# Clustered attention, mixture of experts and a rational layer on one core: first logits kept in PSUM, early weight loads and routing steps placed anew

## The chip, the cores and the metric

The kernel runs on one core of a Trainium2 chip. Its engines are TensorE (PE; the loads of its stationary operand are listed as PEld), VectorE (DVE), ScalarE (ACT), GpSimd (POOL) and SyncE (SP), which issues most DMAs. The metric is the time of one execution on the device, in microseconds (us). All texts below count from the first instruction of the profiled execution.

## The reference: what is computed

Three layers follow each other; all values are float32.

```python
# 1. attention: B=2, H=8, S=768, D=64, 16 clusters for each head
q_assign = argmax(normalize(q) @ normalize(centroids).T)   # likewise k_assign
scores = where(q_assign[:, None] == k_assign[None, :], q @ k.T / sqrt(D), -1e9)
x = softmax(scores) @ v                                    # to [1536, 512]
# 2. top-1 mixture of experts: E=8, d=512, f=1024
e = argmax(normalize(x) @ normalize(expert_emb).T / tau)
x = gate * (relu(x @ w1[e]) @ w2[e])
# 3. a layer of 2048 with a rational function P/Q between its products
h = x @ w_in
out = (P(h) / (Q(h) + 1e-6)) @ w_out
```

## The kernel before

Every product with weights is made of three matmuls in fp32r: a value is split in a rounded high part and a remainder, and high x high, high x low and low x high are added. The split of a weight chunk (1 MB, `[128, 4, 512]`) goes by quarters: `split_to` (L108) casts the quarter on ScalarE (L110) and subtracts on VectorE (L113).

**The blocks.** The program is written in three blocks under `tc.manual_schedule()`: attention (L642 to L812), experts (L1058 to L1102) and last layer (L1167 to L1192). Within a block each engine's instructions are issued as they are written. The timeline shows that instructions of a later block can be issued ahead of an earlier block's.

**Attention.** 16 heads of two halves make 32 *units*; a unit has 6 *slots*, one for each block of 128 keys, so the loop at L778 has 192 slots and a tail of 6. In a slot TensorE transposes three 128x128 blocks of probabilities (`transp`, `pt`, L428), ScalarE and VectorE split them (`phi` L436, `plo` L446), and TensorE multiplies with values (`pv`, L456 and L457). Other work is put into slots by hand with `at(slot, function)`: the scores of a later unit (`scores`, L410 and L411, then the maximum `nm`, L413, and `expo`, L419), the preparation of a later head, and the storing of `w_in` and `w_out` in another order by way of `words` (word_load, word_low, word_high, word_join, word_store). At the end of a unit `finish` multiplies with an identity and the expert embeddings (`px`, L488).

**A head's preparation.** With w = 12 i - 29 for head i: at slot w - 4 `prep_split` splits keys and queries and starts two moves between partitions (`KB<-QA`, `QB<-KA`); at w + 1 `prep_swap` starts two more, of which the second (`QA<-QA`) overwrites what the first (`KA<-QA`) reads; the clusters' logits, maxima and one-hot follow (`cl_logits` to `cl_onehot`), and at w + 14 `cl_transp` transposes the one-hot and moves it into the operands (`KB<-ot`, `QB<-ot`), where it adds the mask to the scores, which begin at w + 21. All of these moves are DMAs within the chip and go through SyncE's queue, which is in order.

**The start.** The first two heads are prepared ahead of the loop (L696 to L712). Their logits `pl` (`cl_logits_first`, a PSUM tile under the tag of `pt`) are copied to SBUF by ScalarE (`cl_copy_first`, L338); VectorE then subtracts the maximum (L357), scales and adds an index (L359), takes the maximum again (L367) and subtracts (L371). `cl_transp_first(0)` transposes the one-hot of head 0; ScalarE copies it to `KB` and VectorE to `QB` (L395).

**Weights of the experts.** `plan` has 32 chunks, four for each expert: w1 in two halves, then w2 in two halves. `weights(count)` (L161) issues loads into one of three raw buffers (`wraw`, L123) up to two chunks ahead of the one being split, and splits `count` quarters. In the attention loop `weights(0)` is put at slot 130: three loads, no split. The second block begins with `load_x(0)` (the gather of the first expert's rows, a DMA by GpSimd, L842), `weights(8)` (chunks 0 and 1, with the loads of 3 and 4) and `transpose_x(0)`. Chunk 1's ring buffer is that of `words` until the last word is read.

**Routing.** When three blocks of tokens are finished, `route(b, g)` (L511), a generator of nine steps, finds their experts, ranks and rows. `advance()` (L637) takes the first running generator one step on: once in a unit (the slot with kb = 2), twice in each slot from 186 on. In a step the rank matmul reads `cum`, the count by expert so far; the ninth step multiplies `at_row` with `J` (`rJ`, from GpSimd) into `ptab` and adds to `table` and `cum`. The table gives the gather its row numbers (`row_tok`).

**Experts.** For each expert and pair p of 128 columns: `expert_in` (24 matmuls, L959), `weights(3)`, `expert_relu` (ACT L966, DVE L968), `expert_out` of the pair before (L982 to L984), `weights(3)`.

Of the kernel before, what the change touches and what calls it, by code (L numbers as in the profile page):

```python
# [10 lines left out]
F32 = mybir.dt.float32  # L11
# [10 lines left out]
P = 128  # L22
# [6 lines left out]
def attention_moe_kernel(ctx: ExitStack, tc: tile.TileContext, kqT, vp, centroids,  # L29
# [37 lines left out]
    def move(dst, src):  # L67
        sp.dma_start(dst.bitcast(F32), src.bitcast(F32))
# [51 lines left out]
    def prep_f32(key, src, tag):  # L120

        raw = stage.tile([P, 4, 512], F32, name="wraw", tag="wraw")
        sp.dma_start(raw, src)  # L123
        yield
        ck = new_chunk(key, tag)
        for i in range(4):
            split_to(ck, i, raw[:, i], act, dve)
            yield
# [29 lines left out]
        e, c = divmod(n - RING, 4)  # L158
        return n < RING or (("in", "in", "out", "out")[c], e, 2 * (c % 2) + 1) in passed

    def weights(count):  # L161

        while place["chunk"] < len(plan):
            n, ahead = place["chunk"], place["loaded"]
            if ahead < len(plan) and ahead <= n + 2:
                next(plan[ahead])
                place["loaded"] += 1
                continue
            if count == 0 or not free(n):
                return  # L170
            next(plan[n])
            count -= 1
            place["quarter"] += 1
            if place["quarter"] == 4:
                place["chunk"] += 1
                place["quarter"] = 0

# [118 lines left out]
    def prep_swap(i):  # L298
        hi, lo = st[i]["QA"], st[i]["KA"]
        move(lo[D:P], hi[0:D])  # L300
        move(hi[0:D], hi[D:P])

    def prep_split_first(i, qk):
# [27 lines left out]
    def cl_logits_first(i):  # L331
        pl = pT.tile([P, NB, 2 * C], F32, name="pl1", tag="pt")
        for blk in range(NB):
            pe.matmul(pl[:, blk, :], st[i]["kq"][:, blk * P:(blk + 1) * P], CB[:, heads[i][1], :],
                      start=True, stop=True)
        st[i]["pl"] = pl

    def cl_copy_first(i):  # L338
        st[i]["L"] = hp.tile([P, G, C], F32, name="L")
        act.copy(st[i]["L"].rearrange("p (b a) c -> p b (a c)", a=2), st[i].pop("pl"))  # L340

    def cl_logits(i):
        pl = pM.tile([P, NB, 2 * C], F32, name="pl", tag="pm")
# [6 lines left out]
    def cl_max(i):  # L350
        st[i]["mx"] = sm.tile([P, G, 1], F32, name="mx")
        dve.tensor_reduce(st[i]["mx"], st[i]["L"], axis=AX.X, op=ALU.max)
# [35 lines left out]
    def cl_transp_first(i):  # L388

        po = [pS.tile([C, 1024], BF16, name="po1", tag="ps") for a in range(2)]  # L390
        for a in range(2):
            for blk in range(NB):
                pe.transpose(po[a][:, blk * P:(blk + 1) * P], st[i]["ohb"][:, blk, a, :], identb)
        act.copy(KBs[i % NSET][0:C], po[0][:, :S])  # L394
        dve.tensor_copy(QBs[i % NSET][0:C], po[1][:, :S])  # L395
# [115 lines left out]
    def route(b, g):  # L511
# [45 lines left out]
        rk = rE("rrk")  # L557
        dve.tensor_tensor(rk, oh, pr, op=ALU.mult)
        dve.tensor_reduce(rank, rk, axis=AX.X, op=ALU.add)
        yield  # L560

        second = r3("rsec")
        dve.tensor_scalar(second, rank, float(P), None, op0=ALU.is_ge)
        row = r3("rrow")
        dve.scalar_tensor_tensor(row, second, -float(P), rank, op0=ALU.mult, op1=ALU.add)
        at_row = xpool.tile([P, 3, P], F32R, name="at_row", bufs=1)
        dve.tensor_tensor(at_row, iotp.unsqueeze(1).to_broadcast([P, 3, P]),
                          row.to_broadcast([P, 3, P]), op=ALU.is_equal)
        J = xpool.tile([P, 3, E, 2], F32R, name="rJ")
# [5 lines left out]
               pM.tile([P, E * 2], F32, name="ptab", tag="pm"))  # L575
        for j in range(3):
            pe.matmul(pt_, at_row[:, j, :], J[:, j].rearrange("p e t -> p (e t)"), start=(j == 0), stop=(j == 2))
        cs = xpool.tile([P, E], F32, name="rcs")
        dve.tensor_reduce(cs, ohb.rearrange("p j e -> p e j"), axis=AX.X, op=ALU.add)
        if last:  # L580
            dve.tensor_tensor(row_tok, table, pt_, op=ALU.add)
        else:
            dve.tensor_tensor(table, table, pt_, op=ALU.add)
        dve.tensor_tensor(cum, cum, cs, op=ALU.add)


    n = len(units)
# [3 lines left out]
    def at(slot, fn, *args):  # L591
        tasks.setdefault(max(slot, 0), []).append((fn, args))
# [3 lines left out]
    for i in range(2, NH):  # L596
        w = (i - 2) * 2 * NB - 5
        if i > 2:
            at(w + -4, prep_split, i)
            at(w + 1, cl_logits, i)  # L600
            at(w + 1, prep_swap, i)
        at(w + 1, cl_max, i)
        at(w + 4, cl_rank, i, dve if i == 2 else pool)
        at(w + 7, cl_first, i)
        at(w + 8, cl_diff, i, dve if i == 2 else pool)
        at(w + 9, cl_onehot, i)
        at(w + 14, cl_transp, i)
        at(w + 16, prep_v, i)
        if i + 2 < NH:
            at(max(w + 7, 9), prep_load, i + 2)  # L610
# [31 lines left out]
    with tc.manual_schedule():  # L642
# [26 lines left out]
        load_v(2)  # L669

        dve.memset(half, 0.5)
        junk = hp.tile([P, DM], F32, name="junk", bufs=1)
        acc = const.tile([P, 4], F32, name="acc")
        make_identity(nc, ident)
        dve.memset(CB, 0.0)
# [16 lines left out]
            pool.memset(t[0:D].bitcast(F32), 0.0)  # L692
        prep_split(1)
        prep_swap(1)
        prep_split_first(0, qk)
        cl_logits_first(0)  # L696
        cl_logits_first(1)
        cl_copy_first(0)
        cl_max(0)
        cl_rank(0, dve)  # L700
        cl_first(0)
        cl_diff(0, dve)
        prep_split(2)
        cl_onehot(0)
        cl_copy_first(1)
        norm_1(embs, E, junk[:E, :], acc[:E, 2:3])
        cl_max(1)
        cl_rank(1, dve)
        cl_transp_first(0)
        cl_first(1)  # L710
        cl_diff(1, dve)
        cl_onehot(1)  # L712
# [8 lines left out]
        expo(0, 2)  # L721
        cl_logits(2)
        prep_swap(2)
        expo(1, 0)

        def rest_1():
# [46 lines left out]
        for slot, fn in ((42, constants_1), (48, constants_2), (61, constants_3), (73, constants_4)):  # L773
            at(slot, fn)
        at(1, prep_load, 3)
        at(130, weights, 0)

        for t in range(T + 6):  # L778
            u, kb = divmod(t, NB)
            todo = tasks.pop(t, [])  # L780
            if t < T:
                transp(u, kb)
            for fn, args in todo:
                if fn is word_high:
                    fn(*args)
            for fn, args in todo:
                if fn is expo:
                    fn(*args)
            if t < T:
                transp_lo(u, kb)  # L790
            if t >= NB and kb == 4 and u - 1 not in FK:
                finish(u - 1)
                i, g = units[u - 1]
                if heads[i][1] == H - 1:
                    begin(route(heads[i][0], g))
            for fn, args in todo:
                if fn is not expo and fn is not word_high:
                    fn(*args)
            if t >= 2 and t - 2 < T and (t - 2) % NB:
                pv((t - 2) // NB, (t - 2) % NB)  # L800
            if t >= NB and kb == 1:
                pv(u - 1, 0)
                pv_out(u - 1)
            if t >= NB and kb == FK.get(u - 1):
                finish(u - 1)
                i, g = units[u - 1]
                if heads[i][1] == H - 1:
                    begin(route(heads[i][0], g))
            for _ in range(2 if t >= T - NB else kb == 2):
                advance()  # L810
        while running:
            advance()  # L812

    px_.close()
    xstack.close()
# [241 lines left out]

    with tc.manual_schedule():  # L1058
        load_x(0)
        weights(8)  # L1060
        transpose_x(0)
        later = [row_gates(0), positions()]
        next(later[0])
        steps = [(e, p) for e in range(E) for p in range(FB // 2)]
# [257 lines left out]
```

## Time and profile before

| | |
|---|---|
| runs | 781.44, 782.83, 788.40 us; median 782.83 |
| profiled execution | 782.98 us, of which the span from first to last instruction is 781.3 |
| mean granted TensorE clock | 0.982 of full |
| PE, PEld busy | 736.7, 643.2 us |
| DVE, ACT, POOL busy | 597.3, 566.2, 352.2 us |
| DMA | 109.22 MB, 140 GB/s in the mean |

A row of the timeline names the start, the duration, engine, line and operation, the tile written and the tiles read, and in brackets how long the engine was idle before and what ended that. "x6" merges six of a kind. A table by windows has, for each stretch, the time in which each engine was busy and its number of instructions, the mean granted clock of TensorE (1.00 is full), and the share of time in which the DMA engines were busy. Waits are listed as who waited for whom, with the sum, the number and the longest.

### The profile page before, as it was taken

How to read it: one execution, taken by the hardware profiler on the slowest of the kernel's cores; microseconds unless marked ns; L12 is line 12 of the kernel's file. 1: busy time of each engine (PE TensorE's matmuls, PEld its weight loads, DVE VectorE, ACT ScalarE, POOL GpSimd, SP SyncE). 2: the span in 40 equal slices, each digit the busy share in tenths (PEclk: the TensorE clock that was granted, in tenths of full speed). 3: DMA queues.
4: the chain of work that ended last, by engine and by line, in shares of the span. 5: the costliest groups of instructions: out<-in, count | busy, mean ns of one | idle time of the engine just before them, and what ended most of it. 6: DMA issues, size and time to landing. Idle time of an engine off the chain costs nothing. (4 is left out here: it accounts for less than half of the span.)

```text
span 781.3 us, 12623 instructions
## 1 busy us (share of the span) xinstructions
PE 736.7 (94%) x4292; PEld 643.2 (82%) x4292; DVE 597.3 (76%) x1120; ACT 566.2 (72%) x1132; POOL 352.2 (45%) x448
## 2 busy tenths in 40 slices
PE   5999999999979975999999999999999999999995
PEld 4799999989869964988999899878788888888884
DVE  7788888889867993888656564598987878787774
ACT  3788888888868862777755565588887777777773
POOL 7498888878765523021110112066544432242212
PEclk9999999999999995999999999999999999999998
DMA  5566776778877332699655746222100200010001
GB/s 150 154 198 177 215 210 185 228 198 264 268 204 212 100 127 81 229 322 314 210 197 201 267 157 219 86 67 96 29 0 11 73 17 11 1 54 1 1 0 58
DMA packets 48313, 109.22 MB, mean 140 GB/s; under 512 B 6921, under 2 KB 10505, under 8 KB 48242
## 3 DMA queue, kind: packets, MB, share of 16 engines
q1 hardware_dynamic: 45042, 97.74, 40.4%
q0 software_dynamic: 3200, 10.60, 4.3%
q8 instruction: 36, 0.59, 0.3%
q14 instruction: 35, 0.29, 0.1%
HBM read 76.06 MB, written 18.99 MB: 122 GB/s over the span
## 5 line engine op out<-in xcount | busy, mean ns | idle before, releaser
L1054 POOL TENSOR_TENSOR Bt<-Bt,A 128x512 f32<-128x512 f32 x46 | 59.6, 1296 | 146.5 <-ACT Bt L1052 146.5
L446 DVE TENSOR_TENSOR plo<-pt,phi 128x384 fp32r<-128x384 f32 x160 | 88.0, 551 | 23.1 <-ACT phi L436 20.7
L436 ACT CAST phi<-pt 128x384 fp32r<-128x384 f32 x160 | 76.7, 483 | 35.4 <-PE pt L428 34.3
L413 DVE TENSOR_REDUCE nm<-ps 128x1 f32<-128x768 f32 x96 | 91.3, 951 | 10.5 <-PE ps L411 10.1
L428 PE MATMUL pt<-ident,pr 128*128 128x128 f32 x576 | 96.6, 277 | 2.4 <-DVE plo L446 2.1
L1027 PE MATMUL pg<-x2hi,ck 128*128 128x512 f32 x368 | 92.5, 393 | 2.4 <-DVE Ct L1055 2.4
L113 DVE TENSOR_TENSOR ck<-wraw,ck 128x512 fp32r<-128x512 f32 x128 | 82.3, 694 | 14.4 <-ACT ck L110 14.4
L419 ACT ACTIVATE pr<-ps,nm 128x768 f32<-128x768 f32 x96 | 87.4, 911 | 1.9 <-DVE nm L413 1.3
L1027 PEld LDWEIGHTS pg<-x2hi,ck 128*128 128x128 f32 x368 | 68.9, 188 | 18.7 <-DVE Ct L1055 3.3
L428 PEld LDWEIGHTS pt<-ident,pr 128*128 128x128 f32 x576 | 72.2, 141 | 14.3 <-DVE plo L446 6.0
L1151 PE MATMUL pr<-ck,ghi 128*128 128x512 f32 x192 | 75.9, 395 | 0.0
L1153 PE MATMUL pr<-ck,glo 128*128 128x512 f32 x192 | 75.4, 393 | 0.0
L1152 PE MATMUL pr<-ck,ghi 128*128 128x512 f32 x192 | 75.1, 391 | 0.0
L110 ACT CAST ck<-wraw 128x512 fp32r<-128x512 f32 x128 | 71.2, 623 | 5.3 <-DMA wraw<-in_w_dram 5.2
L410 PE MATMUL ps<-KA,QA 128*128 128x384 f32 x192 | 74.4, 388 | 0.6 <-ACT KB L394 0.4
L456 PE MATMUL po_acc<-phi,vhl 128*128 128x384 f32 x192 | 74.1, 386 | 0.0
L959 PE MATMUL ph<-xhi,ck 128*128 128x256 f32 x512 | 73.3, 287 | 0.7 <-ACT xhi L946 0.7
L959 PEld LDWEIGHTS ph<-xhi,ck 128*128 128x128 f32 x512 | 69.1, 194 | 3.6 <-ACT xhi L946 1.1
L411 PE MATMUL ps<-KB,QB 128*128 128x384 f32 x192 | 66.9, 348 | 5.3 <-DMA QB<-ot 3.7
L852 POOL TENSOR_TENSOR gss<-gss,half 128x2 f32<-128x2 f32 x8 | 5.8, 721 | 144.4 <-ACT px L851 144.4
L457 PE MATMUL po_acc<-plo,vhl 128*128 128x384 f32 x192 | 65.3, 340 | 0.0
L1128 DVE SCALAR_TENSOR_TENSOR Bt<-Bt,A 128x512 f32<-128x512 f32 (+1 forms) x48 | 32.7, 682 | 37.3 <-ACT A L1127 37.0
(252 smaller groups left out, 1847.1 us busy)
## 6 DMA issues: line engine op xcount, KB each, us to landing
wraw<-in_w_dram SPq DMA_DIRECT2D x32, 1024.0 KB, 6.7
words<-in_w_in_dram SPq DMA_DIRECT2D x16, 512.0 KB, 3.9
wf_d<-wz SPq DMA_DIRECT2D x32, 256.0 KB, 2.3
words<-in_w_out_dram SPq DMA_DIRECT2D x16, 512.0 KB, 6.0
yraw<-wf_d SPq DMA_DIRECT2D x16, 512.0 KB, 3.7
kq<-in_kqT_dram SPq DMA_DIRECT2D x16, 384.0 KB, 4.2
ys_d<-ysb SPq DMA_DIRECT2D x16, 260.0 KB, 6.4
v<-in_vp_dram SPq DMA_DIRECT2D x16, 192.0 KB, 5.4
```

Source lines behind the costliest of these rows:

```text
L113: el.tensor_tensor(ck[:, 1, i], src, ck[:, 0, i].bitcast(F32), op=ALU.subtract)
L410: pe.matmul(o, d["QA"][:, q0:q0 + P], d["KA"][:, nh * HS:(nh + 1) * HS], start=True, stop=False)
L413: dve.tensor_reduce(nm, ps[:, :, :HS], axis=AX.XY, op=ALU.max, negate=True)
L419: act.activation(pr.rearrange("p (a s) -> p a s", a=2), ps[:, :, :HS], AF.Exp, bias=nm[:, 0:1], accum_out=st["sum", u][:, qb:qb + 1])
L428: pe.transpose(t[:, j, :], st["P", u][j][:, kb * P:(kb + 1) * P], ident)
L436: act.copy(phi, tv)
L446: dve.tensor_tensor(plo, tv, phi.bitcast(F32), op=ALU.subtract)
L959: pe.matmul(ph[:, f2, :], w[:, wx, k, c0:c0 + P], x[:, k, :], start=(i == 0), stop=(i == len(ops) - 1))
L1027: pe.matmul(ph, w[:, wx, k, c0:c0 + P], x[:, k, :], start=(i == 0), stop=(i == len(ops) - 1))
L1151: pe.matmul(o, ghi[:, s_], w[:, 0, k, :], start=(fb == 0), stop=False)
L1152: pe.matmul(o, ghi[:, s_], w[:, 1, k, :], start=False, stop=False)
L1153: pe.matmul(o, glo[:, s_], w[:, 0, k, :], start=False, stop=(fb == F2B - 1))
```

## The change

The logits of heads 0 and 1 stay in PSUM, where VectorE works on them in place, and the one-hot of head 0 is transposed ahead of head 1's `cl_rank`. The second move of a swap is issued three slots later. The first three weight loads are issued at slots 131, 143 and 155. Chunk 0 is split at the end of the first block; the second block gathers and transposes x, then issues the load of chunk 3 from ScalarE's queue and splits chunk 1. Two routing generators advance in the same step, and `cum` is brought up to date before the ninth step, except in the last group.

```diff
@@ prep_f32
-        sp.dma_start(raw, src)
+        (act if key == ("w2", 0, 1) else sp).dma_start(raw, src)
@@ weights
-    def weights(count):
+    def weights(count, loads=2):
-            if ahead < len(plan) and ahead <= n + 2:
+            if ahead < len(plan) and ahead <= n + loads:
+    def load_ahead(n):
+        assert place["loaded"] == n
+        next(plan[n])
+        place["loaded"] += 1
@@ prep_swap
         move(lo[D:P], hi[0:D])
+
+    def prep_swap_2(i):
+        hi = st[i]["QA"]
         move(hi[0:D], hi[D:P])
@@ cl_logits_first
-        st[i]["pl"] = pl
-
-    def cl_copy_first(i):
-        st[i]["L"] = hp.tile([P, G, C], F32, name="L")
-        act.copy(st[i]["L"].rearrange("p (b a) c -> p b (a c)", a=2), st[i].pop("pl"))
+        st[i]["L"] = pl.rearrange("p b (a c) -> p (b a) c", a=2)
@@ route
+        def count():
+            cs = xpool.tile([P, E], F32, name="rcs")
+            dve.tensor_reduce(cs, ohb.rearrange("p j e -> p e j"), axis=AX.X, op=ALU.add)
+            dve.tensor_tensor(cum, cum, cs, op=ALU.add)
+
+        if not last:
+            count()
         yield
...
-        at_row = xpool.tile([P, 3, P], F32R, name="at_row", bufs=1)
+        at_row = xpool.tile([P, 3, P], F32R, name="at_row", bufs=2)
...
-        cs = xpool.tile([P, E], F32, name="rcs")
-        dve.tensor_reduce(cs, ohb.rearrange("p j e -> p e j"), axis=AX.X, op=ALU.add)
         if last:
             dve.tensor_tensor(row_tok, table, pt_, op=ALU.add)
+            count()
         else:
             dve.tensor_tensor(table, table, pt_, op=ALU.add)
-        dve.tensor_tensor(cum, cum, cs, op=ALU.add)
@@ preparation of the heads, in the loop over i
             at(w + 1, prep_swap, i)
+            at(w + 4, prep_swap_2, i)
@@ first block
-        junk = hp.tile([P, DM], F32, name="junk", bufs=1)
+        junk = words["z"][5].bitcast(F32)
...
         prep_swap(1)
+        prep_swap_2(1)
         prep_split_first(0, qk)
         cl_logits_first(0)
         cl_logits_first(1)
-        cl_copy_first(0)
         cl_max(0)
...
-        cl_copy_first(1)
         norm_1(embs, E, junk[:E, :], acc[:E, 2:3])
         cl_max(1)
+        cl_transp_first(0)
         cl_rank(1, dve)
-        cl_transp_first(0)
...
         prep_swap(2)
+        prep_swap_2(2)
...
-        at(130, weights, 0)
+        for j in range(3):
+            at(131 + 12 * j, load_ahead, j)
...
-                advance()
+                advance(2)
         while running:
             advance()
+        weights(4, 1)
@@ second block
         load_x(0)
-        weights(8)
         transpose_x(0)
+        load_ahead(3)
+        weights(4)
```

## Rows read from the trace of the kernel before

**Rows 1.** The page: busy time by engine over the span.
```profile
PE 736.7 (94%) x4292; PEld 643.2 (82%) x4292; DVE 597.3 (76%) x1120; ACT 566.2 (72%) x1132; POOL 352.2 (45%) x448
```
**Rows 2.** Busy time by windows: steady attention, its middle, the hand-over.
```profile
core 0: us, PE busy (x) PEld busy (x) DVE busy (x) ACT busy (x) POOL busy (x), PEclk, DMA share, GB/s
39.10:55.10 16.00, 15.99 (x115) 14.90 (x114) 13.53 (x26) 13.89 (x32) 14.68 (x22) 1.00 0.78 228
227.90:250.50 22.60, 18.86 (x115) 17.29 (x116) 13.94 (x29) 13.97 (x32) 14.98 (x24) 0.85 0.74 180
294.60:306.70 12.10, 3.27 (x16) 2.30 (x15) 3.84 (x19) 1.95 (x6) 2.94 (x4) 0.54 0.23 58
```
**Rows 3.** Timeline of TensorE: ends of units, four apart, twice.
```profile
71.20 0.89 PE L488 MATMUL px<-JE,ob 128*128 128x72 f32 x6
...
103.22 0.89 PE L488 MATMUL px<-JE,ob 128*128 128x72 f32 x6
...
208.51 0.68 PE L488 MATMUL px<-JE,ob 128*128 128x72 f32 x5
...
250.45 0.79 PE L488 MATMUL px<-JE,ob 128*128 128x72 f32 x6
```
**Rows 4.** Timeline of ScalarE and of SyncE's queue, 203 to 230.
```profile
214.73 0.63 ACT L110 CAST ck<-wraw 128x512 fp32r<-128x512 f32 x1
...
203.04 1.75 SPq L123 DMA_DIRECT2D wraw<-in_w_dram  x3
...
221.48 0.39 SPq L123 DMA_DIRECT2D wraw<-in_w_dram  x1
...
229.09 0.47 SPq L68 DMA_DIRECT2D QA<-QA  x1
```
**Rows 5.** Waits of SyncE, 212 to 223: sum, times, longest.
```profile
SPq L123 <- DVE rr L473: 5.7, 1, 5.7
```
**Rows 6.** Waits of TensorE, 180 to 250.
```profile
PE ps L411 <- DMA QB<-ot: 3.5, 1, 3.5
PE pt L428 <- DVE plo L446: 1.4, 3, 1.0
PE px L488 <- DVE table L583: 0.8, 1, 0.8
```
**Rows 7.** Timeline of the start, 10 to 20.
```profile
10.06 2.77 PE L334 MATMUL pl<-CB,kq 128*128 128x32 f32 x12 [0.95 <-POOL kq L286]
...
13.56 1.45 PE L393 MATMUL po<-identb,oh 128*16 128x128 bf16 x12 [0.73 <-ACT oh L375]
...
16.70 0.94 DVE L395 CAST QB<-po 16x768 fp32r<-16x768 bf16 x1
...
17.69 0.69 PE L411 MATMUL ps<-KB,QB 128*128 128x384 f32 x1 [1.63 <-DVE QB L395]
...
19.06 0.96 DVE L413 TENSOR_REDUCE nm<-ps 128x1 f32<-128x768 f32 x1
```
**Rows 8.** Instructions of tile L: minimum, median, maximum in ns; first, last start.
```profile
L359 DVE SCALAR_TENSOR_TENSOR L<-L,iotc x3: 357/865/1869, 10.3 to 26.2; 128x192 f32<-128x192 f32 x3
```
**Rows 9.** Instructions of line 446, 40 to 280, the same columns.
```profile
L446 DVE TENSOR_TENSOR plo<-pt,phi x145: 521/557/559, 39.7 to 279.9; 128x384 fp32r<-128x384 f32 x145
```
**Rows 10.** Timeline of the end of attention.
```profile
282.80 0.62 ACT L110 CAST ck<-wraw 128x512 fp32r<-128x512 f32 x1
...
285.79 0.50 PE L577 MATMUL ptab<-rJ,at_row 128*128 128x16 f32 x3 [1.92 <-POOL rJ L571]
...
289.02 0.69 DVE L113 TENSOR_TENSOR ck<-wraw,ck 128x512 fp32r<-128x512 f32 x1
```
**Rows 11.** First expert: timeline; then landing of the loads of line 123.
```profile
312.23 0.60 ACT L966 ACTIVATE hhi<-ph 128x512 fp32r<-128x512 f32 x1 [2.66 <-PE ph L959]
...
312.86 0.69 DVE L968 SCALAR_TENSOR_TENSOR hlo<-ph,hhi 128x512 fp32r<-128x512 f32 x1 [2.40 <-ACT hhi L966]
...
321.00 0.39 PE L982 MATMUL py<-ck,hhi 128*128 128x512 f32 x1
...
335.04 1.35 POOL L842 DMA_INDIRECT xr<-xd,row_tok  x1 [0.87 <-DVE ck L113]
...
DMA to landing us min/median/max: 5.4/6.7/7.3
```

## The prediction

> **What bounds the kernel now.** First the page's busy table [rows 1]: TensorE is busy 94% of the span, and VectorE and ScalarE follow at 76% and 72%. So time can come only from stretches in which TensorE waits or runs below full clock. The stretches are in the busy table by windows [rows 2]: a steady stretch of attention leaves it 0.01 us idle in 16.00, the stretch from 227.9 to 250.5 leaves 3.74 idle at a mean granted clock of 0.85, and the hand-over to the experts (294.6 to 306.7) has 3.27 us of matmul in 12.10. The third view is the timeline of the `px` matmuls, which end a unit (half a head): [rows 3] show 32.02 us for four units in the steady part (71.20 to 103.22) and 41.94 for four units from 208.51 to 250.45. There 9.9 us are lost.
>
> Why, the timeline says [rows 4]. In program order the splitting of the first weight chunks stands behind the whole attention loop, yet the first ACT cast of it runs at 214.73, and the SyncE load of the fourth chunk (`wraw`) starts at 221.48. So the instructions of a later block are issued ahead of an earlier one's when their inputs are there. That load must wait until a raw buffer has been split, and SyncE stood 5.7 us for it [rows 5]. Behind it in the same queue were a head's swap, issued at 229.09, and its one-hot moves; TensorE then waited 3.5 us for `QB<-ot`, its one wait for a DMA between 180 and 250 [rows 6], and the granted clock fell behind it (the mean of 0.85).
>
> **Part by part.** Each sum is against the profiled execution, 782.98 us (a span of 781.3 and 1.7 around it); the median of the three runs is 782.83, so both are the same.
>
> *Loads apart, first chunk at the end of the first block, fourth behind the gather (middle of attention).* The first block now holds the split of chunk 0 as its last items, so by the order within a block it can't be issued early; chunk 1 stands behind the transposes of x, which wait for routing. The fourth load goes to ScalarE's queue behind the same transposes. In the middle therefore go four casts, four subtractions, the 5.7 us of SyncE and the stall with its slow matmuls. Before, the three loads were issued together at 203.04 [rows 4]; now they come 12 slots apart, each two slots behind a head's one-hot moves, and the swap's second move no longer makes SyncE wait ahead of those. The four units don't go back to 32.0, though: the table update of the first routing step group keeps its wait of 0.8 [rows 6] and its matmuls (0.50 each time, by the like in [rows 10]), together 1.3; the second group's now falls here too, another 1.3; and its VectorE steps, beside those of the first group, I estimate at 0.6 over all units concerned. 9.9 - 3.2 = 6.7 us gained. Bounds: 8.6 if only one table update shows, 1.0 if moves still come late.
>
> *Logits in PSUM (start).* The two ACT copies go, and the chain maximum, difference, scaling, maximum, difference works on PSUM. TensorE's order here is logits of head 1, one-hot transposes of head 0, scores. The logits end at 12.83, the transposes took 1.45, the VectorE copy of `QB` 0.94 [rows 7], so the first `L411` matmul, the second of the scores, can start at 15.2 instead of 17.69. That copy ran late because the slow chain of head 1 stood ahead of it (L359 took 1.87 [rows 8]); the changed order puts it in front. The next gate is the maximum of scores (`nm`), which ran at 19.06 behind that chain. With four operations of head 1 left after the copy, at 0.36 each (the fastest L359 [rows 8]), it comes at 16.8. 2.2 us gained. The trace has no operation that writes its result in place in PSUM. One that reads PSUM and SBUF (L446, 384 elements) stays at 0.52 to 0.56 over 145 times, with GpSimd working beside it [rows 9], so I take the fast figure. With the slow figure, 1.87 - 0.36 for L359 and about as much for the differences, nothing is gained: bounds 0 and 2.5.
>
> [...]
>
> *Routing side by side (end of attention).* The second group of batch 0 now runs in units 17 to 25 and no longer in the last units. There TensorE waited 1.92 us for `rJ` and ran 0.50 of `ptab` matmuls [rows 10], with transposes and the last-but-one `px` queued behind. Chunk 1's casts (the first at 282.80) and subtractions leave too; one of these, 0.69 at 289.02, stood in VectorE's queue in the chain of the last routing. 1.92 + 0.50 + 0.69 = 3.1; I take 3.0. What is late next there is the last head's own chain. Bounds: 1.9 (the wait alone) and 3.6.
>
> *Hand-over.* Chunk 0's four casts (0.62 each [rows 10]) and subtractions run while routing ends and the gather is out; ScalarE was busy 1.95 and VectorE 3.84 of those 12.10 us [rows 2], so 2.5 and 2.8 more find room. What is new is that the gather is issued beside such subtractions. The one gather with a subtraction named as its releaser waited 0.87 [rows 11]. I take 0.4. [...]
>
> Chunk 1's four casts and subtractions, about 2.5 and 2.8 us, now stand between the transposes and the first `expert_relu`. ACT was idle 2.66 and VectorE 2.40 there, while TensorE ran the first 24 matmuls below full clock [rows 2, 11]: covered to 0.4 us, and the rest is not needed until the first `expert_out`. Without that cover it is 2.8. The issue of the load on ACT is one more item, for which the trace has no row; between 0 and the 1.35 of GpSimd's gather issue [rows 11], taken as SyncE's 0.4 [rows 4] and hidden there too. Chunk 4's raw data is asked for once chunk 1 is split, by 311 (VectorE's idle time before 312.86 began at 310.5), and lands 5.4 to 7.3 later [rows 11], at 316 to 318; its first cast stands ahead of the second `expert_relu`, whose product TensorE wants at 321.00. With 1.3 for relu and remainder (0.60 and 0.69) that is covered by about 1 us. So 0.4 in all; bounds 0 and 3.
>
> *At nothing:* the buffer lent for `junk`, the earlier count, the second `at_row` buffer. The delayed second move of a swap has 17 slots until its head's scores.
>
> Sum: 782.98 - 6.7 - 2.2 - 3.0 + 0.4 = **771.5 us**.
>
> **Rivals.** *The start gives nothing:* VectorE is as slow on PSUM beside GpSimd. For it, the spread of L359; against it, L446. 771.5 + 2.2 = 773.7.
>
> *The middle stays:* with DMA at 0.78 of its engines' time already in a steady stretch [rows 2], 1 MB more per head makes moves late, or the order in the block isn't kept and chunk 0 is still split at 214. Gain there 1.0 instead of 6.7: 777.2. Against it: the three loads issued together at 203.04 cost TensorE no wait for a DMA by themselves; the only one came behind the fourth [rows 6].
>
> *Three stalls for one:* each load now brings its own late one-hot moves, for the last three heads. One such stall with the slow matmuls behind it cost about 6 us (22.60 against 16.00 [rows 2], less what else waits); three are 18, and the middle loses 11.3 instead of gaining 6.7: 789.5, slower than before. It decides from the second stall on (783.5), where a one-hot move lands over 7 slots, some 9 us, after its transposes. Against it: those moves are issued ahead of the load.
>
> **How the numbers follow.** Forecast 0.62, no gain at the start 0.12, the middle stays 0.21, three stalls 0.05. The bounds taken together reach from 768.3 to 783.1; 767.5 to 780.0 leaves out the stalls, the far ends and little else. What a measurement of this kernel can tell from no change is about 1%, here 7.8 us: faster means below 775.0. That holds for nearly all of the forecast, most of the second case and a little of the third: 0.71. Above 790.7 lies only part of the last case: 0.03. The rest is 0.26.
>
> **What would show it.** Right: no ACT cast of `ck` before the last `px`; no SyncE wait for VectorE in the middle and no TensorE wait for `QB<-ot`; four units from the 21st in about 35 us; the second score matmul near 15.3; the last `px` 11 to 12 us earlier, and the experts' first matmul as far behind it as before. Wrong: L359 above 0.6 us on PSUM, a TensorE wait on a DMA in attention, ScalarE waiting for `wraw` while TensorE idles at 321, or a stage after the hand-over that is longer than before.

## The result, and the profile after

Five executions of the changed kernel took 774.37 to 777.55 us, median 775.55; beside them the kernel before took 781.44 to 788.40, median 782.83 (five). The ratio is 0.9893, interval 0.9863 to 0.9922. The medians differ by 7.3 us, which is 0.93%; by the ratio of all runs the gain is 1.07%, with an interval from 0.78% to 1.37%. So the interval leaves out no change, but the result lies on the 1% limit that the prediction drew: the median is 0.55 us above 775.0. The forecast was 771.5 in a range from 767.5 to 780.0. The result lies in the range and 4 us above the forecast, 7.3 us of gain where 11.3 were forecast; two of the four terms came out otherwise than worked out.

The profiled execution after took 774.37 us, with a span of 772.6, 8.7 less than before. It is the fastest of the five, so the 8.7 us hold about 1.4 more than the medians show. Its line numbers are higher: `L488` is now `L493`, `L411` `L416`, `L413` `L418`, `L359` `L364`, `L577` `L590`, `L583` `L595`, `L842` `L856`, `L959` `L973`, `L982` `L996`; `L110`, `L113` and `L123` stay. The page's busy row answers to [rows 1]: the same work in a shorter span.

```profile
PE 736.3 (95%) x4292; PEld 643.4 (83%) x4292; DVE 595.9 (77%) x1120; ACT 566.1 (73%) x1130; POOL 353.6 (46%) x448
```

Where the 8.7 us lie is read from the starts of each unit's `px` matmuls (units counted from 0). The table is drawn from the two timelines; a negative number means that the changed kernel is ahead.

| at | before | after | ahead | won since the row above |
|---|---|---|---|---|
| unit 0 | 39.11 | 38.86 | -0.25 | -0.25 |
| unit 2 | 55.20 | 54.86 | -0.34 | -0.1 |
| unit 17 | 174.76 | 174.44 | -0.32 | 0 |
| unit 21 | 208.51 | 211.91 | **+3.40** | **+3.7** |
| unit 25 | 250.45 | 246.32 | -4.13 | **-7.5** |
| unit 28 | 272.26 | 268.15 | -4.11 | 0 |
| unit 31 (the last) | 293.70 | 285.98 | -7.72 | **-3.6** |
| first `expert_in` matmul | 306.70 | 299.44 | -7.26 | +0.5 |
| first `expert_out` matmul | 315.36 | 307.27 | -8.09 | -0.8 |
| end of span | 781.3 | 772.6 | -8.7 | -0.6 |

These are rows behind the table, from the timeline of `px` in the changed kernel; they answer to [rows 3].

```profile
211.91 0.89 PE L493 MATMUL px<-JE,ob 128*128 128x72 f32 x6 [1.42 <-DVE rrk L563]
...
228.90 0.89 PE L493 MATMUL px<-JE,ob 128*128 128x72 f32 x6 [0.40 <-DVE table L595]
...
246.32 0.79 PE L493 MATMUL px<-JE,ob 128*128 128x72 f32 x6
```

The four units up to 246.32 now take 34.41 us instead of 41.94. The busy table by windows of the changed kernel (columns as in [rows 2]) shows the same: a steady stretch, the part of the middle that was worst, and the hand-over.

```profile
38.85:54.85 16.00, 15.99 (x115) 14.89 (x114) 13.37 (x26) 14.04 (x32) 14.67 (x22) 1.00 0.74 225
228.90:246.32 17.42, 16.64 (x118) 15.49 (x118) 13.79 (x28) 13.91 (x33) 13.96 (x21) 1.00 0.71 213
286.60:299.40 12.80, 3.90 (x18) 2.76 (x18) 6.33 (x22) 3.96 (x10) 3.70 (x4) 0.50 0.19 51
```

In the middle the clock is 1.00 where it was 0.85, and TensorE is idle 0.78 us instead of 3.74. At the hand-over VectorE and ScalarE now work 6.33 and 3.96 us where they had 3.84 and 1.95: that is chunk 0's split. The waits of TensorE between 180 and 250 in the changed kernel answer to [rows 6].

```profile
PE pt L433 <- DVE plo L451: 1.4, 3, 0.9
PE px L493 <- DVE rrk L563: 1.4, 1, 1.4
PE po L387 <- DVE rrk L563: 0.7, 1, 0.7
PE po L387 <- DVE table L595: 0.5, 1, 0.5
PE px L493 <- DVE table L595: 0.4, 1, 0.4
```

`QB<-ot` is gone. What is left are waits for VectorE: for `plo`, and for `rrk` and `table`, its steps of routing, some of which stood there before ([rows 6] has `table`). The timelines of ScalarE and SyncE answer to [rows 4]: the first cast of `ck` comes behind the last `px`, and each load directly behind a head's swap.

```profile
288.09 2.18 ACT L110 CAST ck<-wraw 128x512 fp32r<-128x512 f32 x4
...
222.28 0.54 SPq L68 DMA_DIRECT2D QA<-QA  x1
222.86 0.58 SPq L123 DMA_DIRECT2D wraw<-in_w_dram  x1
```

### The profile page after: what moved, and what is told of

It is laid out like the page before. It is cut to its first block, busy times and chain, and to the rows that moved or that the text cites. A ratio compares the mean times of both kernels' runs of the same rounds, so it can differ in the third digit from the quotient of the medians.

```text
span 772.6 us, 12619 instructions
## 1 busy us (share of the span) xinstructions
PE 736.3 (95%) x4292; PEld 643.4 (83%) x4292; DVE 595.9 (77%) x1120; ACT 566.1 (73%) x1130; POOL 353.6 (46%) x448
## 5 line engine op out<-in xcount | busy, mean ns | idle before, releaser
L418 DVE TENSOR_REDUCE nm<-ps 128x1 f32<-128x768 f32 x96 | 91.3, 951 | 6.6 <-PE ps L416 6.3
L113 DVE TENSOR_TENSOR ck<-wraw,ck 128x512 fp32r<-128x512 f32 x128 | 80.9, 685 | 13.1 <-ACT ck L110 12.9
L110 ACT CAST ck<-wraw 128x512 fp32r<-128x512 f32 x128 | 70.9, 623 | 7.5 <-DMA wraw<-in_w_dram 7.4
L973 PE MATMUL ph<-xhi,ck 128*128 128x256 f32 x512 | 72.9, 286 | 0.7 <-ACT xhi L960 0.7
L973 PEld LDWEIGHTS ph<-xhi,ck 128*128 128x128 f32 x512 | 68.8, 193 | 3.6 <-ACT xhi L960 1.1
L416 PE MATMUL ps<-KB,QB 128*128 128x384 f32 x192 | 66.8, 348 | 0.1
```

The source lines that it names most:

```text
L113: el.tensor_tensor(ck[:, 1, i], src, ck[:, 0, i].bitcast(F32), op=ALU.subtract)
L418: dve.tensor_reduce(nm, ps[:, :, :HS], axis=AX.XY, op=ALU.max, negate=True)
L973: pe.matmul(ph[:, f2, :], w[:, wx, k, c0:c0 + P], x[:, k, :], start=(i == 0), stop=(i == len(ops) - 1))
```

## The experiments

Twelve kernels were run, all made from the changed kernel. They ran in three groups, each beside its own runs of the kernel before, which took 781.06 to 791.65 us in all; so medians are compared within a group and ratios across groups.

| run | what is altered | median (range, runs), us | ratio to before, interval |
|---|---|---|---|
| changed kernel | | 775.55 (774.37 to 777.55, 5) | 0.9893 [0.9863, 0.9922] |
| e1 | routing groups in turn | 776.13 (775.43 to 777.00, 4) | 0.9882 [0.9820, 0.9945] |
| e2 | second group's steps three slots later | 775.25 (774.63 to 777.20, 4) | 0.9877 [0.9814, 0.9941] |
| e2b | in turn, second group in units 25 on | 775.50 (774.77 to 779.82, 4) | 0.9887 [0.9817, 0.9956] |
| e3 | weights' loads and splits as before | 781.01 (779.28 to 781.72, 10) | 0.9932 [0.9901, 0.9963] |
| e4 | start as before | 776.34 (775.71 to 781.44, 10) | 0.9916 [0.9882, 0.9949] |
| e5 | chunk 0 split early | 775.96 (775.28 to 776.82, 6) | 0.9903 [0.9872, 0.9935] |
| e6 | three loads together | 778.29 (777.62 to 780.66, 10) | 0.9920 [0.9895, 0.9944] |
| e8 | swap's second move at once | 775.50 (775.37 to 776.10, 4) | 0.9889 [0.9839, 0.9938] |
| e9 | TensorE kept busy at the hand-over | 777.85 (775.41 to 779.17, 9) | 0.9911 [0.9877, 0.9946] |
| e10 | fourth group's keys asked for early | 776.79 (775.54 to 778.70, 10) | 0.9902 [0.9868, 0.9937] |
| e11 | e9 and e10 | 779.34 (777.82 to 780.43, 12) | 0.9922 [0.9889, 0.9954] |
| e12 | e11, and TensorE busy at the start | 779.00 (774.23 to 780.32, 12) | 0.9921 [0.9889, 0.9953] |

e1 to e3 are one group (kernel before: median 787.12, 13 runs), e4 to e8 another (783.78, 21), e9 to e12 a third (784.28, 30). The stretches below come from one profiled execution of each kernel.

Two theories stood for the 3.7 us lost in units 17 to 21, where the prediction had estimated 0.6. A: they are the two groups' steps of routing, side by side in VectorE's queue, and the steps can be had for less in other places. B, the rival: the loss has another source, the later second move of a swap or SyncE's queue. For the gain in the middle it was open which part of the edit to the weights carries it; for the start, what takes the lead back.

### Where the routing steps stand: e1, e2, e2b

```diff
 e1
-                advance(2)
+                advance()
 e2: before the last unit the first generator at kb == 2, the second at kb == 5
 e2b
-            for _ in range(2 if t >= T - NB else kb == 2):
-                advance(2)
+            for _ in range(2 if t >= T - NB else (kb == 2 or (kb == 5 and u > 24))):
+                advance()
```

> The changed kernel with one routing generator advanced at a time, as before; all else as changed. Theory A (the second group's VectorE steps beside the first's are what makes units 18 to 21 longer): the px matmuls from the 18th to the 22nd (174.4 to 211.9, 37.5 us in the changed kernel) come in 33.8 us again, as before the change, and the two units ahead of the last go from 12.2 to 14 or 15 us, since the table update of the second group stands there again; time between 1 us faster and 1 us slower than the changed kernel. Theory B (the second move of a swap, issued later, or the queue of SyncE is what makes them longer): 37.5 us stays, and the end of attention is 2 to 3 us longer, so the time is 2 to 3 us longer than the changed kernel.

> The changed kernel with both routing generators running, but the first stepped in the third slot of a unit and the second in the sixth. Theory A: the VectorE steps no longer meet in one slot; 174.4 to 211.9 shrinks from 37.5 to about 35.5 us, the end of attention stays as in the changed kernel, and the time is 1 to 2.5 us shorter. Theory B: nothing changes, within 0.5 us.

> The changed kernel with the two generators one after the other as before, but two steps a unit from the 26th unit on (third and sixth slot), so that the second group is through by the 30th. Theory A: units 18 to 21 take 33.8 us, units 26 to 30 together 1 to 1.5 us more than in the changed kernel, the last two as in the changed kernel: 2 to 3 us faster than the changed kernel. Theory B: units 18 to 21 stay at 37.5, so 0.5 to 1.5 us slower than the changed kernel.

Stretches between `px` starts, in us, from the timelines:

| | units 17 to 21 | 21 to 25 | 25 to 29 | 29 to 31 | 17 to 31 |
|---|---|---|---|---|---|
| before | 33.75 | 41.94 | 29.34 | 13.91 | 118.9 |
| changed | 37.47 | 34.41 | 28.79 | 10.87 | 111.5 |
| e1 | 33.76 | 33.88 | 29.34 | 14.69 | 111.7 |
| e2 | 36.20 | 35.48 | 28.77 | 10.86 | 111.3 |
| e2b | 33.76 | 33.89 | 32.85 | 10.97 | 111.5 |

Taken in turn, units 17 to 21 fall back to 33.76, and the end grows by 3.8. Put into units 25 to 29, the steps cost 3.5 to 4.1 there. The sum from unit 17 to 31 is 111.3 to 111.7 in all four. So A is right on the source of the loss. But its forecasts of a gain both failed: e2 was to be 1 to 2.5 us faster than the changed kernel and e2b 2 to 3, and both have its time. The side by side part moves time and wins none. The timeline of VectorE in the changed kernel shows how the steps cost; below them is the TensorE wait that follows.

```profile
175.84 0.18 DVE L544 TENSOR_REDUCE rm<-rv 128x3 f32<-128x24 f32 x1
175.94 0.17 DVE L537 TENSOR_REDUCE rmx<-x_sb 128x3 f32<-128x24 f32 x1
176.14 0.58 DVE L539 TENSOR_TENSOR rv<-x_sb,rmx 128x24 f32<-128x24 f32 x1
176.65 0.55 DVE L451 TENSOR_TENSOR plo<-pt,phi 128x384 fp32r<-128x384 f32 x1
...
177.25 0.55 PE L433 MATMUL pt<-ident,pr 128*128 128x128 f32 x3 [0.93 <-DVE plo L451]
```

The second group's `L537` and `L539` follow the first's `L544`; `plo`, for which TensorE's transposes wait, is behind all of them. In e1 the same transposes waited 0.22.

### Which part of the weights' edit carries the middle: e3, e5, e6, e8

```diff
 e3: prep_f32, load slots, both weights() calls as in the kernel before
 e5
-        weights(4, 1)            # end of the first block
+        weights(4, 1)            # second block, between load_x(0) and transpose_x(0)
 e6
-            at(131 + 12 * j, load_ahead, j)
+            at(131, load_ahead, j)
 e8
-            at(w + 4, prep_swap_2, i)
+            at(w + 1, prep_swap_2, i)
```

> The changed kernel with the loads and splits of the first weight chunks as before: three loads in slot 130, then the second block begins with the gather, eight quarters and the loads of chunks 3 and 4 by SyncE. Theory: that alone brings the stall back: a SyncE wait of some 5 us for a VectorE split near 220, a TensorE wait for a one-hot move of 3 us, px from the 22nd to the 26th from 34.4 to 40 to 42 us, and 0.5 to 1 us more at the end of attention from chunk 1's splits: 6 to 9 us slower than the changed kernel, at or above the kernel before. Rival (the earlier one-hot moves by the split swap prevent the stall already): px there below 37 us and 1 to 3 us slower than the changed kernel.

> The changed kernel with the split of chunk 0 first in the second block, where it can be issued early, in the middle of attention; the fourth load stays on ScalarE's queue behind the transposes of x. Theory A (the stall comes from SyncE standing before the fourth load, not from the split): casts near 215 to 225, no TensorE wait for a one-hot move, the px from the 22nd to the 26th at 34.4 to 36 us, time 0 to 1.5 us above the changed kernel. Theory B (the split's work on ScalarE and VectorE makes the stretch longer): 38 us or more there, 4 us slower.

> The changed kernel with the three loads in one slot (131) instead of 12 slots apart. Theory A: the spacing is worth little, since the three loads of the kernel before held up nothing by themselves: px from the 22nd to the 26th within 1 us of 34.4, time within 0.7 us. Theory B (the spacing is what removed the stall): a TensorE wait for a DMA there, 3 us or more slower.

> The changed kernel with the second move of a swap in the same slot as the first, as before. Theory: SyncE stands 2 to 4 us for each again, ahead of the one-hot moves, and these still land in time: time within 0.7 us, no TensorE wait for a DMA over 0.5 us. Rival: with 1 MB loads behind them the one-hot moves come late near 220 to 245, 1 to 3 us slower.

e3 is 4.9 to 5.8 us slower than the three kernels of its group: the edit to the weights carries most of the gain. In its profile 5.3 us more lie in units 21 to 25 and 2.0 in units 29 to 31 (12.83 against 10.87), while units 17 to 21 take 0.9 less (36.61). In e3 SyncE stands 4.6 us for a VectorE subtraction again, and the fourth load starts at 221.22. But TensorE has no wait for `QB<-ot`, and units 21 to 25 take 39.69 all the same: neither the theory's wait for a one-hot move nor the rival's 37 us. Its busy table by windows, and behind it the wait in question, show why.

```profile
222.00:226.00 4.00, 4.00 (x29) 3.74 (x28) 4.00 (x10) 3.05 (x7) 2.44 (x6) 1.00 0.98 310
226.00:230.00 4.00, 1.98 (x16) 1.70 (x14) 2.17 (x6) 2.39 (x7) 3.75 (x6) 0.97 0.41 81
230.00:234.00 4.00, 4.00 (x16) 3.90 (x17) 2.40 (x6) 1.50 (x4) 3.58 (x6) 0.50 0.93 214
234.00:238.00 4.00, 4.00 (x20) 3.83 (x20) 2.23 (x4) 2.87 (x6) 2.60 (x4) 0.67 0.96 269
...
PE px L493 <- DVE table L595: 2.0, 1, 2.0
```

TensorE stood 2.0 us, this time for the table update, and then ran at a mean of 0.50 and 0.67 of its clock for two stretches of 4 us: 16 and 20 matmuls, where the first row has 29.

e6, with the loads together and nothing split early, has the same in smaller: units 21 to 25 in 37.42, 3.0 more than the changed kernel, and the time 2.0 to 2.8 above the other kernels of its group, between what its two theories named and with no wait for a DMA on TensorE. The chain can be followed through three engines' timelines of e6.

```profile
223.26 0.68 POOL L207 TENSOR_SCALAR wz<-words 128x512 f32<-128x512 f32 x1 [2.68 <-DMA words<-in_w_in_dram]
...
228.12 0.59 POOL L368 TENSOR_TENSOR L<-L,iotc 128x192 f32<-128x192 f32 x1
...
228.75 0.35 DVE L372 TENSOR_REDUCE m<-L 128x12 f32<-128x192 f32 x1 [1.35 <-POOL L L368]
...
229.88 0.16 DVE L595 TENSOR_TENSOR table<-table,ptab 128x16 f32<-128x16 f32 x1
...
230.09 0.89 PE L493 MATMUL px<-JE,ob 128*128 128x72 f32 x6 [1.85 <-DVE table L595]
```

GpSimd waited 2.68 us for words of `w_in`. Their load was issued at 209.03, no later than in the changed kernel (209.35), but with three chunks ahead of it instead of one, and it took 14.2 us to land, where the trace of the changed kernel has 4.8 for words in this stretch. Its cluster steps came late (`L368` at 228.12; in the changed kernel at 224.64), VectorE waited for them with the table update behind, and TensorE's `px` waited for that; the clock then was 0.62 from 230 to 234. e5 has the loads apart and the split early (first cast at 212.01, so order between blocks is not kept, as read from [rows 4]): no such stand, 35.58, and a time 0.5 above e8's in its group, inside the spread. e8 gives the changed kernel's ratio: the delayed swap is worth nothing that can be told. So loads apart is the part that counts (3.0), the early split costs 1.2, and e3's 5.3 in these units is 1.1 more than both. The fourth load on SyncE's queue, which only e3 has, was not run by itself; whether the 1.1 belongs to it is open.

### What takes the start's lead back: e4, e10

```diff
 e4: cl_copy_first back, cl_transp_first(0) behind cl_rank(1, dve)
 e10
         load_v(2)
+        prep_load(3, v=False)
...
-        at(1, prep_load, 3)
+        at(1, load_v, 3)
```

> The changed kernel with the start as before (ScalarE copies the logits of heads 0 and 1 to SBUF, the one-hot of head 0 is transposed after head 1's rank). Theory (the start's lead is real and is taken back while GpSimd works off what it gets from head 3's keys and queries on): the second score matmul again near 17.7 instead of 14.8, the first px at 38.5 to 39.5, and the third px at 54.8 to 55.4 as in the changed kernel; the time within 0.7 us of it. Rival (the lead is worth its 2 us, only the low clock of that one execution hid it): 2 us slower.

> The fourth head group's keys are asked for at the start, before the first unit, instead of in slot 1; their values stay in slot 1. Theory: the changed start is early by 2 us where its first unit begins, and gives it back by the third, because GpSimd's split of these keys waits for their data (its wait for the key chunk stands at 2.4 us in the changed kernel) and its sums come late from then on. Then px of the third unit begins at 52 to 53.5 us instead of 54.9, that wait of GpSimd is gone, and the time is 773 to 774.5. Rival: GpSimd has too much to do in these units whatever comes when, or the early load delays the first three: px of the third unit within 0.5 us of 54.9, and the time 775 to 776.5.

With the old start unit 2 begins at 55.45 instead of 54.86, and the time is 0.4 to 0.8 above that of e5 and e8 in its group, inside the spread of either: the start is worth some 0.6 at most that can be told, not 2.2. Yet the chain itself is as fast as forecast. These rows of the changed kernel's timeline answer to [rows 7].

```profile
10.63 0.37 DVE L364 SCALAR_TENSOR_TENSOR pl<-pl,iotc 128x192 f32<-128x192 f32 x1
...
14.76 0.69 PE L416 MATMUL ps<-KB,QB 128*128 128x384 f32 x1
...
16.12 0.96 DVE L418 TENSOR_REDUCE nm<-ps 128x1 f32<-128x768 f32 x1
...
21.33 2.60 PE L350 MATMUL pl<-CB,kq 128*128 128x32 f32 x12
```

The second score matmul comes 2.9 us earlier and `nm` 2.9. In this execution, though, TensorE stayed at its lower pace until 26.8 (the 12 matmuls of `L350` take 2.60 us; before, with the pace risen at 22.2, 1.42), and unit 0 is only 0.25 ahead. In eight other runs with this start (e1, e2, e2b, e3, e5, e6, e8, e9) unit 0 began at 36.2 to 37.0; in e1 the pace had risen at 18.2. Even so their unit 2 begins at 53.8 to 55.0: in e1 the two units take 18.4 us instead of 16.0. There GpSimd's split of the fourth group's keys starts at 31.74 after 5.0 us idle, where before it started at 32.26, and VectorE waits 2.3 us for a sum (`ssum`) that stands behind it in GpSimd's queue. So the rows read as if a lead over those keys is lost again there; e10 is the test of it.

e10 asks for the keys early, and its theory falls: unit 2 at 56.36, 1.5 later than in the changed kernel. The timelines of GpSimd and VectorE in e10:

```profile
27.11 0.84 POOL L292 TENSOR_SCALAR kq<-kq 64x768 f32<-64x768 f32 x1
28.03 0.83 POOL L71 TENSOR_SCALAR QA<-kq 128x768 fp32r<-128x768 f32 x1
28.94 1.85 POOL L299 TENSOR_TENSOR KA<-kq,QA 128x768 fp32r<-128x768 f32 x1
...
28.07 3.00 DVE L747 TENSOR_SCALAR early<-early,acc,itau 8x512 f32<-8x512 f32 x2
```

GpSimd's wait is gone. But its three operations now run beside VectorE's scaling of the embeddings, which takes 3.00 us; in the changed kernel (`L746`, at 30.18) it takes 0.98. TensorE waited 2.8 for it, and its clock was 0.77 and 0.80 from 30 to 38: from 33.1 to 34.7 its matmuls of 384 columns follow each other by 0.32 us, from 35.6 on by 0.17 to 0.18. The two operations took 1.06 and 2.01 us; the second ended at 31.07, 0.3 behind GpSimd's subtraction of 1.85 us (28.94 to 30.79). That the one held up the other is the author's reading of these times. So the early keys traded one wait for another, and that the keys take the lead back is not shown by an experiment: whether it would last if those two did not meet was not tried.

Nor is a lead that lasts through attention kept to the end. In e8's profile the last `px` begins at 284.96, 1.0 ahead of the changed kernel and 2.4 ahead of e10 (287.40), and the first `expert_out` at 306.34 against e10's 308.68. These are the next transposes of an expert's rows that wait for VectorE's `ptot`, from the timelines of e8 and e10.

```profile
344.79 0.66 PE L958 MATMUL px<-ident,xr 128*128 128x128 f32 x4 [2.89 <-DVE ptot L945]
...
344.82 0.66 PE L959 MATMUL px<-ident,xr 128*128 128x128 f32 x4 [0.59 <-DVE ptot L946]
```

Both stand at the same time again, and the spans are 774.4 and 774.2.

### The hand-over: e9, e11, e12

e9 adds 18 matmuls behind the last routing transposes, e12 another 15 at the start; nobody reads their results.

```diff
 e9, end of the first block
+        fill_2(18)    # pe.matmul(t, onesb, onesb, 512 columns) into an unread PSUM tile
 e11: e9 and e10
 e12: e11, with fill(9) ahead of the first heads' preparation, fill(3) twice in it
```

> Adds 18 matmuls of 512 columns, whose result nobody reads, on TensorE behind the last routing transposes, while the tokens are gathered. Theory: the first chunk's first 24 matmuls take 4.84 us because the clock stands at its lower level when they begin, TensorE having idled through the gather; kept at work, they take 3 to 3.4 us, and the time is 773.5 to 775. Rival: the added matmuls run at the lower level too and push the transposes of the tokens back, or the weights' landing sets the pace: the first chunk's first block ends no earlier, and the time is 775.5 to 777.5.

> Both: the fourth group's keys asked for at the start, and 18 matmuls that nobody reads behind the last routing transposes. By the two theories the gains add: 771 to 773.5. By the rivals 775 to 777.

> As the run with both, and 15 more matmuls of 512 columns that nobody reads at the start, around the preparation of the first heads, so that TensorE is at work before its first products. Theory: the clock then rises before 18 us in each execution, px of the first unit begins at 36.5 us or earlier (38.9 in the changed kernel's profile), and the time is up to 1 us under the run with both. Rival: the first unit's begin is set by the first chunks' landing and the chain of VectorE, or the third unit takes the lead back: px of the third unit as in the run with both, and the time within 0.5 us of it.

e9 did what was meant where it was meant: the clock is 1.00 from 295 to 310, the second 24 matmuls begin 3.2 us behind the first instead of 4.9, and the first `expert_out` begins at 305.07 instead of 307.27. The kernel is no faster all the same: ratio 0.9911 against 0.9893, with intervals that overlap. The profiled executions, 776.1 us of span against 772.6, differ by more than that, but the changed kernel's is its fastest. This is the timeline of e9 some 45 us into the experts, ScalarE and TensorE:

```profile
340.30 1.67 ACT L110 CAST ck<-wraw 128x512 fp32r<-128x512 f32 x3 [5.18 <-DMA wraw<-in_w_dram]
...
345.47 1.07 PE L965 MATMUL px<-ident,xr 128*128 128x128 f32 x4 [3.15 <-DVE ptot L952]
```

And this the changed kernel's:

```profile
338.15 1.66 ACT L110 CAST ck<-wraw 128x512 fp32r<-128x512 f32 x3 [3.61 <-DMA wraw<-in_w_dram]
...
343.54 0.66 PE L958 MATMUL px<-ident,xr 128*128 128x128 f32 x4 [0.71 <-DVE ptot L945]
```

ScalarE waits for a chunk, VectorE's subtraction waits for the cast, `ptot` stands behind that, and TensorE waits for `ptot`: 0.7 us in the changed kernel, 3.2 in e9, 3.5 in e11 and in e12. From 300 to 350 the DMA engines are busy 0.88 of the time and move 296 GB/s in the changed kernel, 0.80 and 283 in e9. The rows read as if the stream of chunks sets the pace there and a TensorE that starts 2.2 us earlier waits for it, as e8 does; no run changed the stream, so this is not shown.

The `expert_out` that begins at 349.7 in the changed kernel begins at 353.2 in e9, but that is no measure of what the added matmuls cost: in e1, e4, e8 and e10, which don't have them, the transposes behind `ptot` begin at 344.7 to 345.6 too, and 343.54 is the earliest of all. From the last `px` to the end the changed kernel's profile has 486.6 us, and e1, e2, e2b, e4, e6, e8 and e10, which have the same code there, 486.8 to 489.4. Why the chunk at 340.30 comes later than the changed kernel's at 338.15 is open; the chunk cast at 315.27 was already later (313.98), though SyncE's loads at 302 and 306 were issued 0.5 earlier than there.

In e12 unit 0 begins at 40.62, in e11 at 41.42; TensorE waits 2.8 us for VectorE's scaling in both, as in e10, and the medians are 0.3 apart, so the added matmuls at the start win nothing that can be told. Nor did they bring the rise before 18 us: at 384 columns the matmuls still follow each other by 0.32 us up to 17.55.

No version beat the changed kernel by more than the spread.

## Why the prediction was right, and where it was not

The result fell into a range of 12.5 us whose upper end stands for a gain of 3 us. The forecast inside it was 4 us off, by two terms that failed and one that did better than forecast.

**The middle (6.7): the mechanism was right, its size and its neighbour were not.** Chunk 0's casts, SyncE's 5.7 us, the wait for `QB<-ot` and the slow clock went, and units 21 to 25 took 34.41, against "about 35". By itself the stretch gave 7.5. The step that failed is "I estimate at 0.6 over all units concerned" for the second group's VectorE steps: they cost 3.7 in units 17 to 21, because they stand in one queue with `plo` and the maxima. Net 3.8 instead of 6.7. And naming the one wait for `QB<-ot` was too narrow: e3 and e6 lose 5.3 and 3.0 us in the middle with no wait for that move. So the argument that three loads issued together hold nothing up by themselves does not stand: in e6 they cost 3.0 us, by way of late words. What the spacing of the loads takes away is a burst behind which the next load is late (14.2 us to land in e6, 4.8 in the changed kernel); TensorE then stood some 2 us and paid for it again with the clock (0.62 for 4 us in e6).

**The start (2.2): right on PSUM, wrong on what is late next.** `L364` took 0.37 us in PSUM beside GpSimd's subtraction, where [rows 8] has up to 1.87 from SBUF, and `nm` came at 16.12 against a forecast of 16.8. In the same kernel's third head it took 0.36 from SBUF. The step that failed is the sentence that `nm` is the gate, by which its lead would reach the end. It reached 0.3 to 0.6 us: in this execution the clock rose later, and where it rose early, part of the lead was gone by unit 2 (0.2 to 1.4 us are left there against 55.20) and what e8 had left went behind attention. That GpSimd's keys take it in the first units is what the rows suggest, not what an experiment shows. The rival by which the start gives nothing was near in its time, by another mechanism than its own.

**The end of attention (3.0).** Measured 3.6: units 28 to 31 take 17.83 instead of 21.44. Right as a term; but e1 shows that it is the same time which units 17 to 21 paid. As a pair, forecast at 3.0 less 0.6, the side by side steps are worth nothing. Nor does the part for chunk 1's subtractions (0.69) show by itself: in e1, which has them out of the way, units 28 to 31 take 22.21, no less than before. What is left of these terms is the weights.

**The hand-over (0.4 lost).** Measured 0.46 to the first `expert_in` matmul. As expected the gather is issued beside chunk 0's subtractions; these rows are from the changed kernel's timeline.

```profile
291.85 2.49 DVE L113 TENSOR_TENSOR ck<-wraw,ck 128x512 fp32r<-128x512 f32 x4
291.95 1.74 POOL L856 DMA_INDIRECT xr<-xd,row_tok  x1 [1.37 <-DVE cum L569]
293.99 1.23 POOL L856 DMA_INDIRECT xr<-xd,row_tok  x1 [0.30 <-issue]
...
298.81 0.42 ACTq L123 DMA_DIRECT2D wraw<-in_w_dram  x1
```

The two issues took 1.27 and 1.00 before: they are 0.70 longer together, about one subtraction (0.69 in [rows 10]), so the gather did pay more than the 0.4 and other steps gave some back. The load on ScalarE's queue took 0.42 against an assumed 0.4. ScalarE waited 2.7 us for a chunk at 313.98, and TensorE not at all, as the cover of "about 1 us" said. Not forecast were 0.8 us won right behind it (the clock rose some 4 us into the first expert instead of nearly 6) and 0.6 later, where TensorE's wait for `ptot` is 0.7 instead of 1.3; the latter is inside the scatter of that stretch.

In sum, ahead of the hand-over 7.7 us were won instead of 11.9: 1.9 are missing at the start and 2.9 in units 17 to 25, 0.6 came on top at the end; so the last `px` came 7.7 earlier, not the 11 to 12 that were named as a sign. *Three stalls for one* didn't come, as its counter-argument had it: the moves stand ahead of each load. *The middle stays* didn't either: the stretch gained 7.5 and not 1.0.

## What to carry to other kernels

A lead counts only up to the next resource that does not move with it: before adding a term, look for the next input that comes at its own time (here, by the rows, GpSimd's keys at 31 and the weight chunks after 300) and ask what the engine ahead would wait for. Independent steps put side by side cost, here on an engine with little room, what they saved where they had stood; compare the whole stretch, not the place that got shorter. Three large loads issued at once were paid for by a load behind them (14.2 us to land instead of 4.8), so spacing them was worth 3.0 us though the trace of before showed another wait. And a stretch that differs by 2 us between two profiled executions may do so with the same code: compare more runs before giving it a cause.

## What the runs showed of the hardware that was not expected

- The rise of TensorE's pace at the start varies between executions with the same work: near 18 us in e1, at 26.8 in the changed kernel's profile. The clock column reads 1.00 from 8 to 26 us in both, while in e12 it reads 0.50 from 10 to 18; the pace is seen in the matmuls, which follow each other by 0.32 us at 384 columns below the rise and by 0.17 to 0.18 above it.
- A stand of TensorE of about 2 us in full work (e3, e6) was followed each time by 4 to 8 us at a mean granted clock of 0.50 to 0.67.
- VectorE's two `tensor_scalar` operations of 0.53 us each took 1.06 and 2.01 beside GpSimd's work (e10), while VectorE's operations in PSUM kept to 0.34 to 0.37 beside the same kind of work.
